# Two entries moved in a hand-written order: a scatter on GpSimd goes behind a weight split, a mask on VectorE goes behind a subtraction

## The chip, the core and the metric

One core of a Trainium2 chip runs the kernel. The metric is the device time of one execution in microseconds (us). The kernel before took 399.46 us (median of 3 runs, 399.36 to 399.62).

## The reference

Attention through a memory of 32 slots per head, and behind it a mixture of experts in which each row goes to one expert. All of it is float32; there are 8 batches of 8 heads, 576 rows, head size 64; the expert layer has width 512, 8 experts and 1024 hidden columns.

```python
a = exp(phi - max(phi, axis=rows)); a = a / (sum(a, axis=rows) + 1e-9)
k_m = einsum('bhsm,bhsd->bhmd', a, k); v_m = einsum('bhsm,bhsd->bhmd', a, v)
attn = softmax(q @ k_m^T / 8); x = (attn @ v_m) as 4608 rows of 512
logits = x @ w_gate; expert = argmax(logits); gate = softmax(logits)[expert]
out[row] = gate * (relu(x[row] @ w1[expert]) @ w2[expert])
```

## The kernel before

The 8 batches (0 to 7 in the code) go through the same stages and overlap: while TensorE is in the second expert layer of one batch, the other engines prepare the attention of the next. For each batch the kernel makes `phi`'s softmax and the memories `kvm` (line 308), turns the queries (`qT`, line 1029), makes the scores `sT` (line 451), their softmax and its transpose `eT` (lines 411 to 435), and from `eT` the gate's logits `lg` (line 494). A whole batch is then sent through one expert, the one that most of its rows choose, and its weights are loaded by a register's value. The rows that chose another expert, the strays, are written to lists in DRAM by indirect stores (one for each of the 5 row tiles of a batch, `send_stray`, line 610, GpSimd) and are done again at the end of the kernel.

The expert's matmuls run in pairs of a high and a low part. A second-layer tile of weights is loaded raw (`wraw`), ScalarE copies it to a rounded `whi`, and `wlo = wraw - whi` is the low part (`split`, lines 618 and 619; on GpSimd for most tiles, on VectorE for the rest). TensorE forms `whi*hh + wlo*hh + whi*hl` (line 768). In the first layer the weights are first multiplied with the value memory (`pu`, line 387, two PSUM buffers for each half of the hidden columns), ScalarE rounds each buffer to `uh` (line 391) and VectorE takes `ul = pu - uh` (line 394). PSUM has four buffers for such products, so a `pu` buffer can be written again only when its `uh` and its `ul` have been made.

What stands in which place is written by hand: `ORDER` is a list of step names, a batch digit and a step, and every engine issues its own instructions in the order in which the list makes them ("kept in order", at the end of the function). Nothing reorders them. The steps that matter here:

- `0Y0` to `0Y4`: the indirect stores of batch 0's strays, one row tile each, GpSimd.
- `1W3`: the split of the last second-layer tile of batch 1, `whi` on ScalarE and `wlo` on GpSimd.
- `20K3`, `21K3`: the softmax's subtraction of the row maximum for the two groups of heads of batch 2 (line 415); group 0's on GpSimd, group 1's on VectorE. `20L`, `21L` are the exponentials (line 418, ScalarE), `21M2` the scaling on GpSimd (line 432), `20M3`, `21M3` the transposes to `eT` (line 435, VectorE), `2R` the logits (line 494, TensorE).
- `1o03`: the second-layer product of row tile 0 with the weight tile of `1W3`.
- `3X2`: `stray_hot` of batch 3 (lines 565 and 567, VectorE): `hist` and the mask `soh`, which `3X5` on GpSimd reads (line 593).
- `3UH10`, `3UL10`, `3UH00`, `3UL00`: `uh` and `ul` of the first two `pu` buffers of batch 3, made by `3U0`; `3U1` makes the next two.

Of the kernel before, what the change touches and what calls it, by code (L numbers as in the profile page):

```python
# [31 lines left out]
0o41 0o22 0X2 0X5 10N 20C 2D 0o42 0o43 0y4 0z 1D2 1D1 3L1 1D3 3LQ 0o23 0y2 1U0 1UH00 1UH10 1UL10 1UL00 2E 1U1 1UH11  # L32
1UL11 1UH01 1UL01 1X5 1i00 1i01 1e01 1e00 0X6 0Y0 1i03 1e03 2FV 20F 21F 1i02 1e02 1i13 1e13 1i05 2G 2V 2G1 2V1 1W0
1i17 1e17 1W1 2J 20K1 21K 1e05 2V2 1i04 20K 1W2 00N 1i06 1e06 0Y3 1i16 1e16 1i07 1e07 21K1 20K2 21K2 1e04 21K3 20K3
0Y2 1W3 3L0 21L 21M 21M0 31A 20L 2V3 20M 20M0 20M1 20M2 21M1 1i11 1e11 20M3 31Q 1i12 1e12 21M2 21M3 21N 1o00 0align28
1o01 0align54 1o10 0align80 1o11 0align97 1o02 1o03 1o12 1o13 1y1 1i10 0CE1 1e10 2R 2R1 2R2 1i14 1e14 1i15 1o30 2R3 2X
2X3 2R4 2R6 2LW 1o31 1e15 2S1 1o32 1o33 2D1 1y3 2D3 1o20 1o21 1o22 1o40 1o41 30A 2T1 30A1 31A1 3A2 30B 2X4 30C 30Q 31B
0Y4 20N 1y0 2X2 2X1 31C 3D 1X6 2D0 2U0 2UH00 2UL00 2S0 2T0 2X5 2X6 2UH10 3E 1o42 1o23 2W3 30F 31F 2UL10 1o43 3FV 2i02
# [2 lines left out]
0align5 2o01 41A 2W2 0align31 2o02 0align57 2o03 31K1 2e12 31K2 31K3 30L 30M 2i16 2i15 2i10 0align108 2o10 30M0 2y0  # L41
30M1 31L 31M 31M0 30M2 30N 2e10 41A1 31M1 31M2 0Y1 31N 40A 30M3 2o11 2o12 31M3 3R 3R1 3R2 2i14 2o13 2e16 3R3 2o40 3X3
2y1 2o30 2o31 3R4 3R6 2e14 2e15 40A1 4A2 41B 2o20 2o21 2o32 2o33 2o22 3LW 3S0 3T0 3D0 3D1 40B 3X 2y3 3X4 3D3 5L0 3D2
40C 41C 4D 3X1 2Y2 3S1 3T1 41Q 40Q 2o41 2o42 2o43 2y4 2z 3U0 3UH10 3X2 0CZ 1Y3 3UL10 3UH00 3UL00 3W0 3X5 4E 41F 4FV
40F 3U1 3UH01 3UL01 3UH11 2o23 2y2 4G 4G1 4V 3i13 3UL11 3i15 3e15 3i02 3e13 3X6 3i03 4J 4V1 4V2 3e02 40K 40K1 40K2
3i01 40K3 3e03 4V3 3e01 41K 3i04 3i10 3e04 3W1 50A 41K1 3i06 3e06 3i05 3e05 3e10 3i00 3e00 41K2 3W2 2Y1 40L 40M 5LQ
50Q 3i11 3e11 3W3 40M0 40M1 3i16 3e16 3i07 3e07 41K3 41L 41M 3o00 0align0 3o01 0align26 3o02 3i14 3e14 0align65 3o10
# [1171 lines left out]
```

## Time and profile before

| | |
|---|---|
| median of 3 runs | 399.46 us (399.36 to 399.62) |
| the profiled execution | 399.74 us |
| span of that execution, first to last instruction | 398.1 us |
| mean granted TensorE clock | 0.998 of full speed |
| TensorE (PE) busy | 389.6 us, 98% of the span |
| VectorE (DVE) busy | 272.6 us, 68% |
| ScalarE (ACT) busy | 183.9 us, 46% |
| GpSimd (POOL) busy | 178.1 us, 45% |

The profile is one execution, taken by the hardware profiler. Its own time is 1.6 us longer than its span, and 0.28 us above the median of the runs. In a timeline each row has the start and the duration in us, the engine, the line, the operation, the tile written, the tiles read, and in brackets how long the engine had been idle before and what ended that. `PEld` is TensorE's weight load, which overlaps its matmuls. Matmuls are pipelined, so a matmul's duration is longer than the distance to the next one, and it is the distances between starts that tell whether TensorE lost time.

### The profile page before, as it was taken

The page shows a single profiled execution, that of the slowest core. Times are in us where ns is not written, and L with a number is a line of the kernel's source. Part 1 is how long each engine was busy: PE and PEld are TensorE (multiplying, and loading weights), DVE is VectorE, ACT ScalarE, POOL GpSimd, SP SyncE. Part 2 cuts the span into 40 slices and gives each one's busy share as a digit, 9 for nine tenths or more (in the row PEclk, how much of TensorE's full clock was granted, in tenths as well). Part 3 has the DMA queues.
Part 4 walks back from the last instruction along what each step waited for, and adds up shares of the span by engine and source line. Part 5 has one row for each costly group of instructions (what it writes and reads, how often), then busy time and mean ns, then how long its engine had stood idle before and what let it go on. Part 6 is the DMA issues. An engine that isn't in the chain of part 4 may idle for free.

```text
span 398.1 us, 11110 instructions
## 1 busy us (share of the span) xinstructions
PE 389.6 (98%) x4109; PEld 311.1 (78%) x4109; DVE 272.6 (68%) x719; ACT 183.9 (46%) x516; POOL 178.1 (45%) x268
## 2 busy tenths in 40 slices
PE   8889999999999999999999999999999999999995
PEld 4459777887877988798778887798788988698873
DVE  6899888578765866679646758668665876753313
ACT  3268433572357524664427534484337731371220
POOL 5358713367024530655312973364333747656010
PEclk9999999999999999999999999999999999999999
DMA  8998978991592947883487915787169114868313
GB/s 249 361 391 321 292 260 266 349 384 47 170 349 66 356 183 219 308 280 130 116 278 260 366 37 194 255 274 265 58 210 327 51 29 153 302 194 297 108 29 85
DMA packets 51032, 88.26 MB, mean 222 GB/s; under 512 B 7130, under 2 KB 15966, under 8 KB 50976
## 3 DMA queue, kind: packets, MB, share of 16 engines
q1 hardware_dynamic: 47552, 82.55, 61.2%
q0 software_dynamic: 2752, 4.75, 3.4%
q8 instruction: 35, 0.57, 0.6%
q10 hardware_dynamic: 672, 0.21, 0.2%
q14 instruction: 21, 0.17, 0.1%
HBM read 71.22 MB, written 16.48 MB: 220 GB/s over the span
## 4 chain that ended last, share of the span: by engine, by line
PE 75%; POOL 1%; DVE 0%; issue 0%
PE py L768 37%; PE ph L714 20%; PE py L667 6%; PE pu L387 3%; PE kvm L308 3%; PE sT L451 2%; PE lg L494 1%; POOL wlo L619 1%; PE py L653 1%; PE spy L938 0%; PE sph L918 0%; PE px L658 0%; PE sx L906 0%; POOL stray_list L610 0%; PE pk L346 0%; PE pg L367 0%
## 5 line engine op out<-in xcount | busy, mean ns | idle before, releaser
L768 PE MATMUL py<-whi,hh 128*128 128x512 f32 x256 | 101.3, 396 | 0.0
L768 PE MATMUL py<-wlo,hh 128*128 128x512 f32 x256 | 100.0, 391 | 0.2 <-POOL wlo L619 0.2
L768 PE MATMUL py<-whi,hl 128*128 128x512 f32 x256 | 99.8, 390 | 0.0
L648 DVE SCALAR_TENSOR_TENSOR hl<-ph,hh 128x224 fp32r<-128x224 f32 (+1 forms) x128 | 51.9, 416 | 42.4 <-ACT ht L645 25.7
L714 PE MATMUL ph<-eh,uh 128*128 128x288 f32 x252 | 77.2, 306 | 0.0
L714 PE MATMUL ph<-eh,ul 128*128 128x288 f32 x252 | 74.3, 295 | 0.0
L714 PE MATMUL ph<-el,uh 128*128 128x288 f32 x252 | 74.2, 295 | 0.0
L619 POOL TENSOR_TENSOR wlo<-wraw,whi 128x1024 fp32r<-128x1024 f32 x25 | 60.4, 2426 | 28.8 <-ACT whi L618 21.8
L645 ACT ACTIVATE hh<-ph 128x224 fp32r<-128x224 f32 (+1 forms) x128 | 47.7, 387 | 26.9 <-PE ph L714 26.4
L768 PEld LDWEIGHTS py<-whi,hh 128*128 128x128 f32 x256 | 48.0, 188 | 11.3 <-issue 2.0
L768 PEld LDWEIGHTS py<-whi,hl 128*128 128x128 f32 x256 | 48.0, 188 | 10.3
L768 PEld LDWEIGHTS py<-wlo,hh 128*128 128x128 f32 x256 | 48.1, 188 | 9.6 <-POOL wlo L619 0.6
L610 POOL DMA_INDIRECT stray_list<-pay,posi x40 | 42.1, 1053 | 23.5 <-issue 9.0
L714 PEld LDWEIGHTS ph<-eh,uh 128*128 128x128 f32 x252 | 47.3, 188 | 6.2 <-issue 1.2
L714 PEld LDWEIGHTS ph<-eh,ul 128*128 128x128 f32 x252 | 47.3, 188 | 0.3
L714 PEld LDWEIGHTS ph<-el,uh 128*128 128x128 f32 x252 | 47.3, 188 | 0.0
L783 ACT ACTIVATE y<-py,gw 128x512 f32<-128x512 f32 x31 | 21.2, 688 | 46.6 <-issue 27.4
L618 ACT CAST whi<-wraw 128x1024 fp32r<-128x1024 f32 x32 | 33.7, 1058 | 0.0
L553 POOL COPY gw<-gw 64x1 f32<-64x1 f32 x8 | 1.9, 236 | 68.6 <-DVE gw L547 68.6
L394 DVE TENSOR_TENSOR ul<-pu,uh 128x512 fp32r<-128x512 f32 x32 | 20.9, 682 | 16.3 <-ACT uh L391 16.2
L291 ACT ACTIVATE pT<-pT,nm 128x288 f32<-128x288 f32 x32 | 16.8, 528 | 11.8 <-DVE nm L286 11.8
L667 PE MATMUL py<-whi,ht 128*128 128x512 f32 x56 | 21.9, 391 | 0.0
(215 smaller groups left out, 586.9 us busy)
## 6 DMA issues: line engine op xcount, KB each, us to landing
wraw<-in_moe_w_dram SPq DMA_DIRECT2D x66, 512.0 KB, 5.9
kv<-in_v_dram SPq DMA_DIRECT2D x16, 576.0 KB, 7.6
out_dram<-y SPq DMA_DIRECT2D x141, 64.0 KB, 3.0
kv<-in_k_dram SPq DMA_DIRECT2D x14, 576.0 KB, 7.4
qt<-in_q_dram SPq DMA_DIRECT2D x10, 576.0 KB, 9.8
pt<-in_phi_dram SPq DMA_DIRECT2D x15, 288.0 KB, 6.4
ad<-s_t POOLq DMA_DIRECT2D x15, 288.0 KB, 3.5
sw<-in_moe_w_dram SPq DMA_DIRECT2D x6, 512.0 KB, 7.0
```

The costliest lines, as they stand in the source:

```text
L291: nc.scalar.activation(out=pT[:, j], in_=pT[:, j], func=AF.Exp, bias=nm[:, g, j:j + 1], scale=1.0, accum_out=zp[:, g, j:j + 1])
L308: nc.tensor.matmul(kvm[s][o0:o0 + 32, 0:2 * D], lhsT=as_[g][s0, j, c, :], rhs=kvs[g][s0, :, j, c, :], start=(c == 0), stop=(c == C - 1))
L394: nc.vector.tensor_tensor(out=ul[:, g, n0:n0 + DM], in0=pu[g, n0], in1=uh[:, g, n0:n0 + DM].bitcast(F32), op=ALU.subtract)
L610: nc.gpsimd.indirect_dma_start(out=ld_list[i][:, :], out_offset=bass.IndirectOffsetOnAxis(ap=posi[:, i:i + 1], axis=0), in_=pay[:, i, :], ...
L618: nc.scalar.copy(out=hi, in_=raw)
L619: eng.tensor_tensor(out=lo, in0=raw, in1=hi.bitcast(F32), op=ALU.subtract)
L645: nc.scalar.activation(out=hi, in_=ph, func=AF.Relu)
L648: nc.vector.scalar_tensor_tensor(out=lo, in0=ph, scalar=0.0, in1=hi.bitcast(F32), op0=ALU.max, op1=ALU.subtract)
L667: nc.tensor.matmul(o, lhsT=l, rhs=r, start=start, stop=stop)
L714: nc.tensor.matmul(ph, lhsT=lhs[:, g, fs], rhs=rhs[:, g, s0:s1], start=(n == 0), stop=(n == 5))
L768: nc.tensor.matmul(py, lhsT=lhs[:, f, i * P:i * P + P], rhs=rhs[:, f % 2, :], start=(f == 0 and n == 0), stop=(f == KF - 1 and n == 2))
L783: nc.scalar.activation(out=y, in_=v["py", i], func=AF.Copy, scale=gate)
```

## The change

Two entries of `ORDER` move. `0Y2` stood ahead of `1W3` and now stands behind it. `3X2` stood between `3UH10` and `3UL10` and now stands behind `3UL10`. Nothing else is changed.

```diff
-0Y2 1W3 3L0 21L 21M 21M0 31A 20L 2V3 ...
+1W3 0Y2 3L0 21L 21M 21M0 31A 20L 2V3 ...
...
-... 2z 3U0 3UH10 3X2 0CZ 1Y3 3UL10 3UH00 3UL00 3W0 3X5 4E 41F 4FV
+... 2z 3U0 3UH10 0CZ 1Y3 3UL10 3X2 3UH00 3UL00 3W0 3X5 4E 41F 4FV
```

On GpSimd, in batch 1's second layer (`stray_list` is the target of an indirect store, `s_t` the scores of batch 2):

```order
 L610 DMA stray_list_94<-pay,posi 21504x4
 L415 TENSOR_TENSOR s_t<-s_t,mm_1561 128x576
-L610 DMA stray_list_93<-pay,posi 21504x4
 L619 TENSOR_TENSOR wlo<-wraw_1237,whi 128x1024
+L610 DMA stray_list_93<-pay,posi 21504x4
 L432 TENSOR_TENSOR s_t<-s_t,ssum_1582 128x576
 L440 DMA ad<-s_t 128x576
```

The split now follows directly on the subtraction `20K3`, and the store stands between the split and `21M2`.

On VectorE, where the first layer of batch 3 begins (`y` is the end of batch 2's row tile 4, `hist` and `soh` are the step `3X2`):

```order
 L1029 STREAM_TRANSPOSE qT<-qt 128x1152 x2
 L683 SCALAR_TENSOR_TENSOR y<-py,gw,y 64x512
-L565 SCALAR_TENSOR_TENSOR hist<-em_117,es,hist 128x8
-L567 SCALAR_TENSOR_TENSOR soh<-em_117,es,ohr 128x40
-L394 TENSOR_TENSOR ul<-pu,uh 128x512 x4
+L394 TENSOR_TENSOR ul<-pu,uh 128x512
+L565 SCALAR_TENSOR_TENSOR hist<-em_117,es,hist 128x8
+L567 SCALAR_TENSOR_TENSOR soh<-em_117,es,ohr 128x40
+L394 TENSOR_TENSOR ul<-pu,uh 128x512 x3
 L648 SCALAR_TENSOR_TENSOR hl<-ph,hh 128x224
 L648 SCALAR_TENSOR_TENSOR ht<-ph,ht 128x64
```

Of the four `ul` the first now stands ahead of the two mask instructions, and the other three stay behind them. TensorE, ScalarE and SyncE have the same instructions in the same order as before.

## Rows read from the trace of the kernel before

**Rows 1.** The page: busy time by engine; the chain that ended last.

```profile
PE 389.6 (98%) x4109; PEld 311.1 (78%) x4109; DVE 272.6 (68%) x719; ACT 183.9 (46%) x516; POOL 178.1 (45%) x268
PE 75%; POOL 1%; DVE 0%; issue 0%
```

**Rows 2.** Timeline of all engines around 94 us: start us, us, engine, line, operation.

```profile
93.76 0.39 PE L768 MATMUL py<-whi,hh 128*128 128x512 f32 x1
...
94.44 0.39 PE L768 MATMUL py<-whi,hh 128*128 128x512 f32 x1
...
94.97 0.19 PEld L768 LDWEIGHTS py<-wlo,hh 128*128 128x128 f32 x1 [0.57 <-POOL wlo L619]
94.98 0.50 PE L768 MATMUL py<-wlo,hh 128*128 128x512 f32 x1 [0.15 <-POOL wlo L619]
...
95.54 0.40 PE L768 MATMUL py<-whi,hh 128*128 128x512 f32 x1
```

**Rows 3.** Timeline of POOL, 80 to 100 us.

```profile
88.74 1.04 POOL L610 DMA_INDIRECT stray_list<-pay,posi  x1 [0.30 <-issue]
89.78 1.20 POOL L415 TENSOR_TENSOR s_t<-s_t,mm 128x576 f32<-128x576 f32 x1
91.15 1.33 POOL L610 DMA_INDIRECT stray_list<-pay,posi  x1 [0.18 <-issue]
92.48 2.44 POOL L619 TENSOR_TENSOR wlo<-wraw,whi 128x1024 fp32r<-128x1024 f32 x1
96.42 1.16 POOL L432 TENSOR_TENSOR s_t<-s_t,ssum 128x576 f32<-128x576 f32 x1 [1.50 <-ACT ht L645]
```

**Rows 4.** Timeline of DVE, 86 to 99 us.

```profile
89.10 2.50 DVE L415 TENSOR_TENSOR s_t<-s_t,mm 128x576 f32<-128x576 f32 x1
...
98.94 0.76 DVE L435 STREAM_TRANSPOSE eT<-s_t 128x576 f32<-128x576 f32 x1
```

**Rows 5.** Lines 415 (DVE) and 619 (POOL) over the whole span: duration ns min/median/max.

```profile
L415 DVE TENSOR_TENSOR s_t<-s_t,mm x6: 744/758/2499, 89.1 to 321.3; 128x576 f32<-128x576 f32 x6
...
L619 POOL TENSOR_TENSOR wlo<-wraw,whi x25: 2379/2404/2929, 34.0 to 359.2; 128x1024 fp32r<-128x1024 f32 x25
```

**Rows 6.** Timelines of POOL and DVE in windows between 222 and 229 us.

```profile
222.58 2.40 POOL L619 TENSOR_TENSOR wlo<-wraw,whi 128x1024 fp32r<-128x1024 f32 x1
...
224.94 2.93 POOL L619 TENSOR_TENSOR wlo<-wraw,whi 128x1024 fp32r<-128x1024 f32 x1
...
224.65 0.95 DVE L415 TENSOR_TENSOR s_t<-s_t,mm 128x576 f32<-128x576 f32 x1
```

**Rows 7.** Timeline of PE, 98 to 104 us: the logits of batch 2.

```profile
99.84 0.74 PE L494 MATMUL lg<-eT,gm 128*32 128x160 f32 x16
```

**Rows 8.** Timeline of PE, 164.4 to 166 us: the second products of batch 3.

```profile
164.61 0.59 PE L387 MATMUL pu<-wraw,vT 64*32 64x512 f32 x1
164.62 0.27 PE L308 MATMUL kvm<-kv,pt 64*32 64x128 f32 x1
164.86 1.09 PE L387 MATMUL pu<-wraw,vT 64*32 64x512 f32 x15
165.88 0.50 PE L768 MATMUL py<-whi,hh 128*128 128x512 f32 x1
```

**Rows 9.** Timeline of DVE, 163 to 164.6 us.

```profile
163.20 0.70 DVE L683 SCALAR_TENSOR_TENSOR y<-py,gw,y 64x512 f32<-64x512 f32 x1
163.83 0.21 DVE L565 SCALAR_TENSOR_TENSOR hist<-em,es,hist 128x8 f32<-128x8 f32 x1
163.96 0.25 DVE L567 SCALAR_TENSOR_TENSOR soh<-em,es,ohr 128x40 f32<-128x40 f32 x1
164.13 0.67 DVE L394 TENSOR_TENSOR ul<-pu,uh 128x512 fp32r<-128x512 f32 x1
```

**Rows 10.** Timeline of PE, 211.75 to 213.1 us: the same place in batch 4.

```profile
211.88 0.27 PE L308 MATMUL kvm<-kv,pt 64*32 64x128 f32 x1
211.92 1.09 PE L387 MATMUL pu<-wraw,vT 64*32 64x512 f32 x12
212.94 0.40 PE L714 MATMUL ph<-eh,uh 128*128 128x288 f32 x1
```

**Rows 11.** Timeline of POOL at 169.4 us: the reader of the mask `soh`.

```profile
169.43 0.27 POOL L593 TENSOR_TENSOR pos<-pos,soh 128x40 f32<-128x40 f32 x1
```

More of the change, by code (lines that the diff above doesn't have):

```diff
@@ L34 @@
 1i17 1e17 1W1 2J 20K1 21K 1e05 2V2 1i04 20K 1W2 00N 1i06 1e06 0Y3 1i16 1e16 1i07 1e07 21K1 20K2 21K2 1e04 21K3 20K3
-0Y2 1W3 3L0 21L 21M 21M0 31A 20L 2V3 20M 20M0 20M1 20M2 21M1 1i11 1e11 20M3 31Q 1i12 1e12 21M2 21M3 21N 1o00 0align28
+1W3 0Y2 3L0 21L 21M 21M0 31A 20L 2V3 20M 20M0 20M1 20M2 21M1 1i11 1e11 20M3 31Q 1i12 1e12 21M2 21M3 21N 1o00 0align28
 1o01 0align54 1o10 0align80 1o11 0align97 1o02 1o03 1o12 1o13 1y1 1i10 0CE1 1e10 2R 2R1 2R2 1i14 1e14 1i15 1o30 2R3 2X
@@ L43 @@
 2y1 2o30 2o31 3R4 3R6 2e14 2e15 40A1 4A2 41B 2o20 2o21 2o32 2o33 2o22 3LW 3S0 3T0 3D0 3D1 40B 3X 2y3 3X4 3D3 5L0 3D2
-40C 41C 4D 3X1 2Y2 3S1 3T1 41Q 40Q 2o41 2o42 2o43 2y4 2z 3U0 3UH10 3X2 0CZ 1Y3 3UL10 3UH00 3UL00 3W0 3X5 4E 41F 4FV
+40C 41C 4D 3X1 2Y2 3S1 3T1 41Q 40Q 2o41 2o42 2o43 2y4 2z 3U0 3UH10 0CZ 1Y3 3UL10 3X2 3UH00 3UL00 3W0 3X5 4E 41F 4FV
 40F 3U1 3UH01 3UL01 3UH11 2o23 2y2 4G 4G1 4V 3i13 3UL11 3i15 3e15 3i02 3e13 3X6 3i03 4J 4V1 4V2 3e02 40K 40K1 40K2
```

## The prediction

> **What bounds the kernel now.** I read the page first. TensorE is busy for 98% of the span, and the chain of work that ended last, followed back from the end to 91 us, is TensorE's almost alone; one percent of the span in that chain is GpSimd's [rows 1]. So a change on GpSimd or VectorE pays only where TensorE stands still for it, and then at most what TensorE lost there. The second view is the timeline of TensorE. Behind 90 us I looked for places where two starts lie further apart than the same pair of instructions does elsewhere, and apart from patterns that come back in every batch there are two: one at 94.98 us, which the trace puts down to the split `wlo` on GpSimd [rows 2], and one at 164.86 us, inside the second products of batch 3 [rows 8]. The change touches exactly these two. The third view is the timeline of the engine that TensorE waits for at each, to see what stood ahead of the late instruction.
>
> **The first edit.** What TensorE loses: before the wait its starts lie (94.44 - 93.76) / 3 = 0.227 us apart. The three steps from 94.44 to 95.54 take 1.10 us where 3 x 0.227 = 0.68 would do, so 0.42 us are lost [rows 2]. That is more than the 0.15 us which the bracket gives as idle time, because matmuls overlap and the pipe has to fill again.
>
> Why `wlo` was late: GpSimd ends the subtraction `20K3` at 89.78 + 1.20 = 90.98, then spends 0.18 us on issue and 1.33 us on the store, and begins `wlo` only at 92.48, so that it ends at 94.92 [rows 3]. The weight load wanted it 0.57 us before 94.97, at 94.40 [rows 2]. With the store behind it, `wlo` can start at 90.98. Its inputs are old by then. Alone it takes 2.40 us [rows 5] and would end at 93.38. But it will not be alone: VectorE's subtraction `21K3` stands there from 89.10 to 91.60, 2.50 us for an instruction with a median of 0.76 [rows 4, 5]. It began in the shadow of GpSimd's subtraction and ended 0.62 us behind it, so I read it as waiting for GpSimd, and then running. The nearest rows for what comes next are those at 224 us: two splits stand back to back on GpSimd, VectorE's subtraction arrives 0.33 us before the first ends (222.58 + 2.40 = 224.98), it runs first and ends at 225.60, and the second split takes 2.93 instead of 2.40 us [rows 6]. Taking that value, `wlo` ends at 90.98 + 2.93 = 93.91, still 0.49 us before 94.40, and `21K3` ends at 91.60 as before. The stall goes: **-0.42 us**. Bounds: 0 if the time is lost again at the next thing that is late (below), and 0.42 at most, since TensorE cannot gain more here than it lost.
>
> What the store costs in its new place: with 0.18 us of issue and 1.04 to 1.33 us [rows 3] it runs from about 94.1 to at most 95.4. The next GpSimd instruction, the scaling `21M2`, had stood idle for 1.50 us and started at 96.42 because of something else [rows 3], so the store fits into that idle time: 0 us. If that cover were gone, it would be 1.3 us on the way to `eT`. Its list is read at the end of the kernel only. Nothing else is on that queue behind it except `21M2`.
>
> What is late next: the logits of batch 2. Their second half reads the last `eT` transpose, which ends at 98.94 + 0.76 = 99.70 [rows 4]. The 16 matmuls start over some 0.67 us from 99.84 on [rows 7], so the second half starts at about 100.17, and 0.42 us earlier it would be 99.75. That is only 0.05 us of slack, an estimate from these rows; the gain just fits.
>
> **The second edit.** Here the second buffer of `3U1` waits: the first matmul starts at 164.61, the next ones at 164.86, and the first subtraction `ul` ends at 164.13 + 0.67 = 164.80, 0.06 us earlier [rows 8, 9]. From the last `kvm` matmul to the next matmul that is not `pu` it takes 165.88 - 164.62 = 1.26 us; at the same place in batch 4, where nothing waits, 212.94 - 211.88 = 1.06 us [rows 8, 10]. So 0.20 us are lost. Without the two mask instructions ahead of it, `ul` starts where `hist` did, at 163.83 (0.30 us earlier), and ends at 164.50 [rows 9]. With the same 0.06 us that is 164.56, before TensorE asks at 164.61. The title of the change speaks of two subtractions, but the order shows the mask behind one; since the buffer waited for is that of the first, that is enough. **-0.20 us**; bounds 0 (another reader of the buffer holds it) and 0.25 (the whole distance from 164.61 to 164.86).
>
> The mask itself comes 0.6 us later; its reader on GpSimd starts at 169.43 [rows 11], five microseconds later: 0 us. The second `ul` keeps its place, since the sum of what stands ahead of it is the same.
>
> **The sum.** -0.42 - 0.20 = -0.62 us. The profiled execution would go from 399.74 to 399.12 us. It stands 0.28 us above the median of the runs, so I expect 399.46 - 0.62 = 398.84, say 398.85 us, 0.15% less. Changes within 0.2% (0.8 us) can hardly be told from none with a measurement of this kernel, so "the same" is the likeliest verdict although I expect a real gain.
>
> **The rivals.**
>
> GpSimd goes first, and it gets slower. When `20K3` ends at 90.98, either `21K3` or `wlo` goes on. In the kernel before, the issue gap of 0.18 us behind `20K3` let VectorE in; now a ready instruction of the same kind as `20K3` follows at once. Against VectorE speaks that `21K3` had waited since 89.10 and GpSimd's `20K3` still got in before it at 89.78 [rows 3, 4]; for VectorE speak the rows at 224 us, where the order of the same two kinds is exactly that of the changed kernel. If GpSimd wins, `21K3` ends at 93.38 + 0.62 = 94.00, 2.40 us later. The chain behind it (exponential, sum, scaling, transpose) has no idle time of that size, so `eT` ends at 102.10 and the logits' second half waits from 99.75 until then, 1.93 us behind the 100.17 of before. With the -0.20 of the second edit that is +1.7 us, 401.2 us. It decides from a delay of 0.05 + 0.62 = 0.67 us of `21K3` on: below that there is still a gain. Chance 0.12.
> The Trainium skill ("SBUF — State Buffer", section on the two separate sides of SBUF) has a rule on this: VectorE operations with two SBUF inputs and GpSimd operations share a pair of ports, whichever starts first holds it for its whole instruction, and the other blocks fully. The trace agrees that one blocks (2.50 against 0.76 us), but the rule does not say which of two waiting ones starts first, and so leaves this rival open.
>
> Only a part arrives. The slack of 0.05 us at the logits is less than nothing if the transposes move by a little, and what TensorE wins at 94 us is then given back at 100 us: 399.46 - 0.20 = 399.25 us. Or the buffer of the second products is held by something else, and only the first edit pays: 399.05 us. For it speaks that TensorE runs at 98% and any small wait shows; against it, that most of what it waits for later is released by its own earlier work and moves along. Chance 0.23 together.
>
> More than the sum. The raw tile is freed a microsecond earlier (93.91 against 94.92), so the loads that follow start earlier, and TensorE may find one of its smaller waits gone too. No row shows a wait of that size for such a load behind 90 us, so I give it 0.08; it would be some 398.4 us.
>
> **How the numbers follow.** Both edits pay: 0.57, from 398.55 to 399.05 us with the spread of the runs (0.13 us either way). Faster by over 0.2% means below 398.66: all of the last rival and about a fifth of the forecast's own spread, with something for what I did not see, 0.22. Slower by over 0.2%, above 400.26: GpSimd first, 0.12. The rest, 0.66, is the same. The range goes from 398.35 (more than the sum) to 399.75 (nothing gained, plus the spread of the runs) and leaves out that rival and little else.
>
> **What would show it.** In the profile of the changed kernel GpSimd goes from `s_t` (line 415) to `wlo` (line 619) with no store between, `wlo` takes about 2.9 us and ends near 93.9, and VectorE's subtraction still ends near 91.6. TensorE's starts around 94.7 lie 0.23 us apart with no bracket of `wlo`. The logits start near 99.4. At 164 us `ul` precedes `hist`, and from the last `kvm` to the next product it takes about 1.06 us. I am wrong if VectorE's line 415 ends near 94 and the logits wait for `eT`; if the wait of TensorE moves to another place and the span shrinks by less than 0.3 us; or if the second products still show a step of 0.25 us.

## The result: 2 us slower, by the rival and not by the forecast

The changed kernel took 401.51 us (median of 6 runs, 401.22 to 402.6), the kernel before 399.54 us beside it (6 runs, 399.36 to 399.77): a ratio of 1.0053, with a 95% interval from 1.004 to 1.0066. The forecast was 398.85 us. The rival in which GpSimd goes first, priced at 401.2 us, is what happened. The profiled execution shown here took 402.6 us, with a span of 400.8 us. (One experiment below, the one with no issue ahead, was profiled in an execution 5 us longer at a granted clock of 0.981; its rows are read for order and durations only.)

On the page, TensorE's busy time and the chain that ended last, which answer to [rows 1], hardly tell the two kernels apart. The chain has 2% less of TensorE, and 1% each of VectorE and issue. What stands out is VectorE's busy time, 2.5 us more than before; one subtraction that waits, shown below, makes 2.35 us of it, since its wait counts as busy:

```profile
PE 390.1 (97%) x4109; PEld 310.8 (78%) x4109; DVE 275.1 (69%) x719; ACT 183.6 (46%) x516; POOL 178.0 (44%) x268
...
PE 73%; DVE 1%; issue 1%; POOL 1%; ACT 0%
```

The timeline of TensorE (start us, us, engine, line, operation, and in brackets the idle time before it and what ended it) shows what went and what came:

```profile
94.68 0.39 PE L768 MATMUL py<-whi,hh 128*128 128x512 f32 x1
94.91 0.39 PE L768 MATMUL py<-wlo,hh 128*128 128x512 f32 x1
...
98.53 0.39 PE L768 MATMUL py<-whi,hl 128*128 128x512 f32 x1
99.38 0.37 PE L714 MATMUL ph<-eh,uh 128*128 128x288 f32 x1 [0.46 <-DVE ht L648]
...
100.34 0.47 PE L494 MATMUL lg<-eT,gm 128*32 128x160 f32 x8
102.32 0.47 PE L494 MATMUL lg<-eT,gm 128*32 128x160 f32 x8 [1.52 <-DVE eT L435]
```

The stall that the first edit was aimed at is gone: the product with `wlo` starts 0.23 us behind its neighbour, without a bracket, where [rows 2] had one. But two waits are new. TensorE stands idle for 0.46 us because a first-layer buffer comes free too late, and the logits, one run of 16 in [rows 7], fall into two halves with 1.98 us between their starts.

GpSimd's and VectorE's timelines, which answer to [rows 3, 4], say why:

```profile
88.98 1.02 POOL L610 DMA_INDIRECT stray_list<-pay,posi  x1 [0.30 <-DMA kv<-in_k_dram]
90.03 1.17 POOL L415 TENSOR_TENSOR s_t<-s_t,mm 128x576 f32<-128x576 f32 x1
91.15 2.41 POOL L619 TENSOR_TENSOR wlo<-wraw,whi 128x1024 fp32r<-128x1024 f32 x1
93.73 1.33 POOL L610 DMA_INDIRECT stray_list<-pay,posi  x1 [0.18 <-issue]
...
89.33 4.85 DVE L415 TENSOR_TENSOR s_t<-s_t,mm 128x576 f32<-128x576 f32 x1
...
101.51 0.76 DVE L435 STREAM_TRANSPOSE eT<-s_t 128x576 f32<-128x576 f32 x1
```

VectorE's subtraction `21K3` now takes 4.85 us and ends at 94.18. That is 0.62 us behind the end of `wlo` (91.15 + 2.41 = 93.56), as it ended 0.62 us behind the end of `20K3` before. VectorE stood by for two GpSimd instructions instead of one, and got in where GpSimd made its next pause, 0.18 us ahead of the store. In the kernel before that pause stood directly behind `20K3`, because the store did. By moving the store, the change moved the one opening that VectorE had.

ScalarE's timeline shows how a late subtraction becomes two waits:

```profile
94.26 0.69 ACT L418 ACTIVATE s_t<-s_t 128x576 f32<-128x576 f32 x1 [6.15 <-POOL wlo L619]
...
97.50 0.34 ACT L645 ACTIVATE hh<-ph 128x224 fp32r<-128x224 f32 x1
```

It stands idle for 6.15 us before the exponential of what VectorE subtracted. (The bracket names `wlo`, the last thing to end by the profile; the exponential reads `21K3`'s result.) Behind it on ScalarE's queue stand the copies of the first-layer products, and only when VectorE has used them is the buffer free that TensorE wants at 99 us. The exponential, sum, scaling and transpose follow with nothing to give, and `eT` ends at 102.27.

At the second place, VectorE and then TensorE, which answer to [rows 8, 9]:

```profile
166.32 0.69 DVE L394 TENSOR_TENSOR ul<-pu,uh 128x512 fp32r<-128x512 f32 x1 [0.20 <-ACT uh L391]
166.93 0.21 DVE L565 SCALAR_TENSOR_TENSOR hist<-em,es,hist 128x8 f32<-128x8 f32 x1
...
167.34 0.27 PE L308 MATMUL kvm<-kv,pt 64*32 64x128 f32 x1
167.34 1.13 PE L387 MATMUL pu<-wraw,vT 64*32 64x512 f32 x12
168.40 0.50 PE L768 MATMUL py<-whi,hh 128*128 128x512 f32 x1
```

`ul` precedes `hist`, and from the last `kvm` to the next product it takes 168.40 - 167.34 = 1.06 us, as the prediction wanted. But 1.7 us earlier TensorE's weight loads show a pause that the trace of before does not have:

```profile
165.64 1.71 PEld L308 LDWEIGHTS kvm<-kv,pt 64*32 64x32 f32 x117 [0.38 <-issue]
```

The balance against before goes by starts of TensorE's matmuls, since the idle time in a bracket is less than what is lost. For the buffer's wait it needs one more row of the kernel before, the last product ahead of the logits:

```profile
98.74 0.39 PE L768 MATMUL py<-whi,hl 128*128 128x512 f32 x1
```

Up to the logits it is -0.42 (the stall), +0.71 (the buffer: from the last product to the logits 100.34 - 98.53 = 1.81 us, before 99.84 - 98.74 = 1.10) and +1.71 (the logits: 1.98 us between the halves, where 0.74 - 0.47 = 0.27 is the cost of eight more matmuls), together +2.00 us. The medians differ by 401.51 - 399.54 = 1.97 us.

The two profiled executions differ by more, 400.8 - 398.1 = 2.7 us in their spans. The other 0.7 us lie elsewhere: 0.24 us in the first 21 us, ahead of both places; 0.31 us from the logits to the end of the second place, where the pause costs more than the second edit's 0.20 us gives; and 0.20 us near 336 us, where two weight loads wait 0.27 and 0.24 us for `hh` and `hl` as they don't in the trace of before. What of these the executions without a profile have is not shown.

### The profile page after: what moved, and what is told of

Same layout as the page of the kernel before. It is cut to its first block, busy times and chain, and to the rows that moved or that the text cites. A ratio compares the mean times of both kernels' runs of the same rounds, so it can differ in the third digit from the quotient of the medians.

```text
span 400.8 us, 11110 instructions
## 1 busy us (share of the span) xinstructions
PE 390.1 (97%) x4109; PEld 310.8 (78%) x4109; DVE 275.1 (69%) x719; ACT 183.6 (46%) x516; POOL 178.0 (44%) x268
## 4 chain that ended last, share of the span: by engine, by line
PE 73%; DVE 1%; issue 1%; POOL 1%; ACT 0%
PE py L768 36%; PE ph L714 20%; PE py L667 6%; PE pu L387 3%; PE kvm L308 3%; PE sT L451 2%; PE lg L494 1%; POOL wlo L619 1%; PE py L653 1%; PE spy L938 0%; PE sph L918 0%; PE px L658 0%; DVE ssum L422 0%; PE sx L906 0%; DVE eT L435 0%
## 5 line engine op out<-in xcount | busy, mean ns | idle before, releaser
L391 ACT CAST uh<-pu 128x512 fp32r<-128x512 f32 x32 | 17.2, 590 | 10.5 <-PE pu L387 10.4
```

What stands on the lines that cost most here:

```text
L391: nc.scalar.copy(out=uh[:, g, n0:n0 + DM], in_=pu[g, n0])
```

## The experiments

Each is compared with runs of the kernel before on the same chip. The ratios and their 95% intervals are those on record; they are not the quotients of the two medians beside them, and can differ from these by some 0.1%. Two questions: which edit costs the time, and what decides whether VectorE or GpSimd goes first.

**One edit at a time.** First the store alone:

```diff
-... 21K3 20K3 0Y2 1W3 3L0 ...
+... 21K3 20K3 1W3 0Y2 3L0 ...
```

> The first edit alone (the store 0Y2 behind the split 1W3; the mask 3X2 stays where it was before). Theory 'GpSimd runs on': all of the loss comes from this edit, VectorE's subtraction of line 415 near 89 us takes about 4.9 us, the logits of batch 2 wait about 1.8 us for eT, and the time is 2.0 to 2.4 us above the kernel before (0.5 to 0.6%). Rival 'other cause': if the time lies within 0.3 us of the kernel before, the loss needs the second edit or comes from something outside of both places.

Measured: 402.0 us against 399.95, ratio 1.0048 (1.0029 to 1.0066). VectorE's subtraction took 4.82 us and the second half of the logits again waited 1.52 us for `eT`. Then the mask alone:

```diff
-... 3UH10 3X2 0CZ 1Y3 3UL10 3UH00 ...
+... 3UH10 0CZ 1Y3 3UL10 3X2 3UH00 ...
```

> The second edit alone (the mask 3X2 behind 3UL10; the store stays where it was before). Theory: VectorE's ul of batch 3 starts 0.3 us earlier, the step of 0.25 us inside the second products goes, and the time falls by 0.2 us (0.05%), which can hardly be told from none. From the last kvm to the first product that is not pu it takes 1.06 us where it was 1.26. Rival 'another reader holds the buffer': the 1.26 us stay. A loss of over 0.5 us would speak for the second edit as a cause of the slower time.

Measured: 399.77 against 399.95 us, ratio 0.9999 (0.9984 to 1.0014); VectorE's subtraction took 2.50 us as before. So the first edit makes the whole loss, and the second makes nothing that these runs can tell from zero.

**More stores behind the split.** If VectorE is kept out because a store stands ahead, taking away the store ahead (`0Y3`) should let it in:

```diff
-... 1i06 1e06 0Y3 1i16 ... 20K3 1W3 0Y2 3L0 ...
+... 1i06 1e06 1i16 ... 20K3 1W3 0Y2 0Y3 3L0 ...
```

> The changed kernel, with the store 0Y3 moved too: it stood ahead of GpSimd's subtraction 20K3 and now stands behind the split and 0Y2, so that 20K3 and the split 1W3 run back to back with no store ahead of them. VectorE's subtraction 21K3 then arrives in the middle of 20K3, as at 224 us in the kernel before. Theory A 'it is the store ahead of the run that lets GpSimd keep VectorE out': VectorE gets in behind 20K3, its subtraction takes 1.0 to 1.3 us, the split about 2.9 us, both stalls are gone and the time is 0.6 us below the kernel before (0.15%). Theory B 'GpSimd runs on through any row of instructions that are ready': VectorE waits until the split ends near 92.3 us, its subtraction takes about 3.6 us, the logits wait about 0.6 us and the time is 0.4 to 1.0 us above the kernel before.

Measured: 400.4 us, ratio 1.0013 (0.9999 to 1.0028). VectorE was still kept out until `wlo` had ended, at 88.97 + 2.40 = 91.37, plus 0.62:

```profile
87.20 0.62 POOL L440 DMA_DIRECT2D ad<-s  x1
87.85 1.17 POOL L415 TENSOR_TENSOR s_t<-s_t,mm 128x576 f32<-128x576 f32 x1
88.97 2.40 POOL L619 TENSOR_TENSOR wlo<-wraw,whi 128x1024 fp32r<-128x1024 f32 x1
...
88.47 3.52 DVE L415 TENSOR_TENSOR s_t<-s_t,mm 128x576 f32<-128x576 f32 x1
```

So it is not the indirect store as such. What I saw in these rows only later is that now another DMA issue, the plain store of `ad` (step `00N`), stood directly ahead of the run.

**One store between.** The opening put back, with the other store in it:

```diff
-... 1i06 1e06 0Y3 1i16 ... 20K3 1W3 0Y2 3L0 ...
+... 1i06 1e06 1i16 ... 20K3 0Y3 1W3 0Y2 3L0 ...
```

> The changed kernel, with the store 0Y3 moved from ahead of 20K3 to between 20K3 and the split 1W3; 0Y2 stays behind the split. There is again a gap of issue behind 20K3, as in the kernel before, but the split comes one store earlier than there. Both theories A and B: VectorE gets in at that gap, its subtraction takes 1.0 to 1.5 us, the split ends near 93.8 us, 0.6 us before it is wanted, both stalls are gone and the time is 0.6 us below the kernel before (0.15%). If VectorE's subtraction still takes over 3 us, a gap of issue is not what lets it in.

Measured: 399.46 against 399.95 us, ratio 0.9975 (0.9948 to 1.0001).

```profile
87.95 1.17 POOL L415 TENSOR_TENSOR s_t<-s_t,mm 128x576 f32<-128x576 f32 x1
89.30 1.37 POOL L610 DMA_INDIRECT stray_list<-pay,posi  x1 [0.17 <-DMA kv<-in_k_dram]
90.68 2.42 POOL L619 TENSOR_TENSOR wlo<-wraw,whi 128x1024 fp32r<-128x1024 f32 x1
...
88.60 1.15 DVE L415 TENSOR_TENSOR s_t<-s_t,mm 128x576 f32<-128x576 f32 x1
...
98.92 0.74 PE L494 MATMUL lg<-eT,gm 128*32 128x160 f32 x16
```

VectorE gets in at the pause of 0.17 us ahead of the store and ends at 89.75, again 0.62 to 0.63 us behind GpSimd's subtraction; the logits are one run again. `wlo` is early as well, since one store fewer stands ahead of the whole group: this order has the gain without the loss. It was run twice more, first beside a second copy of the kernel before:

> The kernel before, unchanged, with a profile of its own beside those of the variants. The profiles of the changed kernel and of four variants all show a step of 0.4 us inside the kvm matmuls of batch 3 that the first profile of the kernel before does not have. If the step belongs to the execution and not to the edits, it is here too, and the variants are to be compared with this profile. Time: the same as before within 0.2%. VectorE's subtraction near 89 us takes 2.5 us again.

> The version with one store between 20K3 and the split, again, for a tighter interval. Both theories: 0.6 to 1.0 us below the kernel before (0.15 to 0.25%); the logits of batch 2 wait for nothing.

Measured: the copy 399.41 against 399.46 us (0.9999, 0.9974 to 1.0024), the version 398.64 (0.9981, 0.9955 to 1.0008).

> The version with one store between GpSimd's subtraction and the split, once more. By the sum of its parts: VectorE's subtraction of batch 2 takes 1.15 us, no wait in the logits, 0.5 to 0.8 us below before (0.998 to 0.9988). Rival, that the earlier runs were scatter: within 0.2 us of before.

Measured: 399.39 against 399.91 us (0.9994, 0.998 to 1.0009). Its median is lower in all three, by 0.49, 0.82 and 0.52 us, and no interval stands clear of 1. It beats the changed kernel plainly, the kernel before only probably.

**The two instructions by themselves.** A small kernel leaves out the reference's work and stores zeros: GpSimd does a subtraction and two splits back to back, while VectorE's subtraction comes up.

```python
nc.gpsimd.tensor_tensor(out=w, in0=dl, in1=ma.broadcast_to([P, 18, M]), op=ALU.subtract)
for j in range(2):
    nc.gpsimd.tensor_tensor(out=lo, in0=raw, in1=hi.bitcast(F32), op=ALU.subtract)
nc.vector.tensor_tensor(out=s_b, in0=s_b, in1=mb.broadcast_to([P, 18, M]), op=ALU.subtract)
```

> The reference's work is left out; zeros are stored. Twelve cases, one after the other: GpSimd runs a two-input subtraction (short: 576 columns, about 1.2 us; long: 1024 columns, about 2.4 us) and behind it two splits of 1024 columns. VectorE's two-input subtraction of 576 columns (0.76 us alone) arrives while the first one runs. In the cases 'early' the splits have been ready long before; in 'mid' the first split becomes ready, by a copy on ScalarE, only while the first subtraction runs. Theory B1 'GpSimd runs on through what was already waiting in its queue when the present instruction began, and lets VectorE in where the next became ready only later' (it fits 94 us, and 224 us where the split's input was made 0.8 us into the split before): early: VectorE takes 4 to 7 us, until both splits are done, however late it arrives; mid: VectorE gets in behind the first subtraction and takes 0.9 to 2.5 us. Rival B2 'the length or the time of arrival decides' (at 224 us the running instruction was a long one and VectorE came 0.3 us before its end): short: VectorE is kept out, early or mid; long with a late arrival: VectorE gets in, early or mid.

Measured: in all 12 cases VectorE got in behind the instruction that ran when it came, in 1.12 to 2.16 us. Both theories fell, and what was left was a difference between this kernel and the real one: here no DMA issue stood ahead of GpSimd's run. At 224 us of the kernel before, where VectorE got in too [rows 6], none stands directly ahead either. Three experiments put this to the test, each in its own way. The small kernel, with a GpSimd DMA issue ahead:

```diff
+nc.gpsimd.dma_start(out=g, in_=z.rearrange("p t m -> p (t m)"))
 nc.gpsimd.tensor_tensor(out=w, in0=dl, in1=ma.broadcast_to([P, 18, M]), op=ALU.subtract)
```

> The reference's work is left out; the output is zeros. Eleven cases in turn: GpSimd does a short subtraction of two inputs (576 columns) and two splits of two inputs (1024 columns) back to back, and VectorE's subtraction of two inputs comes up while the first of them runs. Ahead of GpSimd's run stands nothing (2 cases), an issue of a plain DMA (4), an issue of an indirect DMA (4), or an issue of a DMA with an idle gap behind it (1). If it is a GpSimd DMA issue directly ahead that keeps VectorE out: with none or a gap VectorE's subtraction takes 1.1 to 2.2 us and the next split 2.8 to 2.9; behind an issue VectorE's ends only with GpSimd's second split, 4 to 7 us, and both splits take 2.3 to 2.4. Rival, that it is not the DMA: all eleven take 1.1 to 2.2 us.

Two cases in the timelines of GpSimd (L83 is the issue, L86 the subtraction, L89 the splits) and of VectorE (L93), with nothing ahead and with an indirect issue:

```profile
6.26 1.16 POOL L86 TENSOR_TENSOR w<-dl,ma 128x576 f32<-128x576 f32 x1 [5.29 <-DVE ma L77]
7.37 5.15 POOL L89 TENSOR_TENSOR lo<-raw,hi 128x1024 fp32r<-128x1024 f32 x2
...
60.21 0.99 POOL L83 DMA_INDIRECT g<-z,idx  x1 [2.96 <-DVE z L72]
61.22 1.18 POOL L86 TENSOR_TENSOR w<-dl,ma 128x576 f32<-128x576 f32 x1
62.34 4.64 POOL L89 TENSOR_TENSOR lo<-raw,hi 128x1024 fp32r<-128x1024 f32 x2
...
6.60 1.43 DVE L93 TENSOR_TENSOR s_b<-s_b,mb 128x576 f32<-128x576 f32 x1
...
61.24 6.37 DVE L93 TENSOR_TENSOR s_b<-s_b,mb 128x576 f32<-128x576 f32 x1
```

With nothing ahead VectorE took 1.43 and 1.42 us. Behind an issue, plain or indirect, it took 5.95 to 6.92 us and ended about 0.62 us behind the second split. Two of the eleven cases test nothing: VectorE took 0.74 us in each, because it came before the reduction behind `ma` had ended, which GpSimd's subtraction waits for. To come ahead of that subtraction is not enough by itself:

```profile
50.46 1.02 POOL L83 DMA_INDIRECT g<-z,idx  x1 [1.68 <-DVE z L72]
...
50.96 6.92 DVE L93 TENSOR_TENSOR s_b<-s_b,mb 128x576 f32<-128x576 f32 x1
```

Here `ma` was done, and VectorE came while GpSimd was still at the issue, 0.54 us ahead of the start of GpSimd's subtraction (51.50); it was kept out all the same. The case meant to have an idle gap had none (0.02 us between issue and subtraction) and took 6.25 us like the others. I had said 4 to 7 us for these.

In the real kernel, no DMA issue ahead: both `0Y3` and `00N` moved behind the split, everything else as in the changed kernel.

```diff
-... 1W2 00N 1i06 1e06 0Y3 1i16 ... 20K3 1W3 0Y2 3L0 ...
+... 1W2 1i06 1e06 1i16 ... 20K3 1W3 0Y2 0Y3 00N 3L0 ...
```

> Change, with batch 0's third store and the plain store of its scores' copy (the line of ad) also moved behind the split, so that GpSimd issues no DMA shortly ahead of its subtraction and the split. If a DMA issue directly ahead keeps VectorE out: VectorE's subtraction of batch 2 takes about 1.0 us, the split about 2.9 instead of 2.4, the second half of the logits does not wait, and the time is 0.3 to 0.7 us below before (ratio 0.998 to 0.999). Rival, that any run of ready instructions in this place keeps VectorE out: its subtraction takes 3.5 us or more, as with three behind, and the time is 0.3 to 1.0 us above before (1.001 to 1.0025).

Measured: 399.43 against 399.92 us, ratio 0.999 (0.9969 to 1.001).

```profile
93.11 1.16 POOL L415 TENSOR_TENSOR s_t<-s_t,mm 128x576 f32<-128x576 f32 x1 [0.34 <-DVE mm L411]
94.23 2.93 POOL L619 TENSOR_TENSOR wlo<-wraw,whi 128x1024 fp32r<-128x1024 f32 x1
...
93.97 0.92 DVE L415 TENSOR_TENSOR s_t<-s_t,mm 128x576 f32<-128x576 f32 x1
```

These are the numbers that the prediction had taken from 224 us: VectorE in 0.92 us, the split in 2.93. The order of the two instructions is the changed kernel's; what stands ahead differs. (GpSimd was idle for 0.34 us ahead of its subtraction: a run with no issue directly ahead begins behind idle time, here as in the small kernel, so the two are one condition in these runs.) And the reverse, in the kernel before: a store put ahead of two of the three splits at 224 us.

```diff
-4e12 51K1 4W1 4W0 5V2 ... 1Y0 3Y3 4Y3 ...
+4e12 51K1 4W1 3Y3 4W0 5V2 ... 1Y0 4Y3 ...
```

> Before, with one store of batch 3 moved from behind GpSimd's three splits of 220 to 228 us to between the first and the second of them. If a DMA issue ahead keeps VectorE out of what follows: VectorE's subtraction there (0.95 us in before, in between the second and third split) ends only with the third split, about 3.5 to 4.5 us, and the third split takes 2.4 instead of 2.9; batch 5's softmax is late by about 2.5 to 3 us and the time is 1 to 2.5 us above before (1.0025 to 1.006). Rival: VectorE still gets in behind the split that runs when it comes (0.9 to 2.5 us), and the time is within 0.5 us of before.

Measured: 402.56 against 399.92 us, ratio 1.0075 (1.0053 to 1.0096), 2.64 us where I had put 1 to 2.5. GpSimd, VectorE, TensorE:

```profile
222.35 1.07 POOL L610 DMA_INDIRECT stray_list<-pay,posi  x1 [0.16 <-issue]
223.43 4.74 POOL L619 TENSOR_TENSOR wlo<-wraw,whi 128x1024 fp32r<-128x1024 f32 x2
...
224.22 4.59 DVE L415 TENSOR_TENSOR s_t<-s_t,mm 128x576 f32<-128x576 f32 x1
...
231.41 0.50 PE L768 MATMUL py<-whi,hh 128*128 128x512 f32 x1 [1.37 <-DVE hl L648]
```

The subtraction that took 0.95 us in [rows 6] takes 4.59, and TensorE waits 1.37 us for `hl`, which stands behind it on VectorE's queue. The last small kernel asks what ends the effect:

```diff
 nc.gpsimd.dma_start(out=g, in_=z.rearrange("p t m -> p (t m)"))
+nc.gpsimd.memset(y, 0.0)
 nc.gpsimd.tensor_tensor(out=w, in0=dl, in1=ma.broadcast_to([P, 18, M]), op=ALU.subtract)
```

> The reference's work is left out; the output is zeros. Twelve cases as before, a plain GpSimd DMA issue ahead of a short subtraction and two splits (four, in two or three cases), with VectorE's subtraction of two inputs coming up during the first of them; between the issue and the run stands an idle gap of some 0.2 to 1.5 us (1, 2, 3 or 8 short VectorE reductions that GpSimd's subtraction waits behind), a GpSimd memset, or a GpSimd copy of one input. If what an issue leaves behind ends with GpSimd's first idle gap: VectorE gets in at 1.1 to 2.2 us behind an idle gap, and is kept out (4 us or more) behind the memset and the copy; with four splits behind an issue it is kept out until the fourth ends, 9 to 11 us. Rival, that it is a matter of time since the issue: the longer gap, the memset and the copy let it in, and of four splits behind an issue it waits for the first two or three only (under 8 us).

Three of its twelve cases (L76 the plain issue, L84 the memset, L89 the subtraction, L92 the splits; VectorE L96): the shortest idle gap, a memset between, and four splits directly behind an issue.

```profile
23.69 0.56 POOL L76 DMA_DIRECT2D g<-z  x1 [2.99 <-DVE z L72]
24.33 1.15 POOL L89 TENSOR_TENSOR w<-dl,ma 128x576 f32<-128x576 f32 x1
...
52.41 0.36 POOL L84 MEMSET y<- 128x288 f32 x1
52.71 1.17 POOL L89 TENSOR_TENSOR w<-dl,ma 128x576 f32<-128x576 f32 x1
...
84.88 1.17 POOL L89 TENSOR_TENSOR w<-dl,ma 128x576 f32<-128x576 f32 x1
85.99 9.22 POOL L92 TENSOR_TENSOR lo<-raw,hi 128x1024 fp32r<-128x1024 f32 x4
...
24.68 1.42 DVE L96 TENSOR_TENSOR s_b<-s_b,mb 128x576 f32<-128x576 f32 x1
...
52.60 6.49 DVE L96 TENSOR_TENSOR s_b<-s_b,mb 128x576 f32<-128x576 f32 x1
...
84.78 11.05 DVE L96 TENSOR_TENSOR s_b<-s_b,mb 128x576 f32<-128x576 f32 x1
```

An idle gap of GpSimd ends it, down to the shortest that was tried: 24.33 - 24.25 = 0.08 us, and VectorE takes 1.42 us, as with nothing ahead; so do the longer gaps. A memset between (6.49 and 6.23 us) or a copy (6.03 us) does not end it. Nor does time: behind an issue VectorE stood by for 11.05 us, until the fourth split was done. All of it is as the first theory said (11.05 us where I had put 9 to 11); the rival, that it is a matter of time since the issue, falls.

## Why the prediction was wrong

**The step that failed** is the one on who goes next at 90.98 us: "the nearest rows for what comes next are those at 224 us". They were nearest in the two instructions and not in what stood ahead of them. At 224 us no DMA issue stood directly ahead of GpSimd's run; at 89.78 the subtraction stood directly behind a store, its start at the store's end [rows 3]. The runs show that this decides: without an issue ahead the changed order gives 0.92 us for VectorE, with one 4.85; and a store put at 224 us turns 0.95 into 4.59. The prediction also misread a row there: `21K3` did not begin "in the shadow of GpSimd's subtraction" but at 89.10, 0.68 us ahead of it, while GpSimd was at the store; so it had lost to an instruction that began later. The right rows stood in the prediction, in the rival: `21K3` had come at 89.10, ahead of `20K3`, and had not been let in, and "the issue gap of 0.18 us" had let it in later. I weighed that against the rows at 224 us and gave it 0.12. As the bounds of that step I took 0 and -0.42, so the unknown order had no end on the side of a loss, though the working of the rival had the price of one.

**The rival's price held.** It gave an end of `21K3` 2.40 us later; 4.85 - 2.50 = 2.35 came. It put the second half of the logits 1.93 us later than before; by the balance it was -0.42 + 0.71 + 1.71 = 2.00. The wait at the buffer I had not seen, because I followed the softmax's chain and not ScalarE's queue behind the exponential. It added nothing of its own: the second half starts 0.05 us behind the end of `eT` (102.32 against 102.27), and VectorE's timeline shows no idle time from 97.63 us up to that transpose, so without the wait at the buffer the one at the logits would have been longer. The rival gave 401.2 us, and 401.51 came.

**The stall behind `wlo`** went as predicted (-0.42), and `wlo` took 2.41 us and not 2.93, since nobody came between. **The late store** cost nothing: the scaling on GpSimd was idle for 3.94 us ahead of its start at 99.00 and still had time. **The slack of 0.05 us** at the logits was not put to the test, by the change or by an experiment: the version with one store between kept the logits in one run with `wlo` early, but there VectorE's subtraction took 1.15 us where it had taken 2.50, so `eT` came earlier too.

**The second edit** did what was said in the order, and `pu`'s step of 0.20 us is not there. Whether it pays is another matter. The pause of 0.35 to 0.38 us in the weight loads of `kvm` stands in the profile of the change and in that of most experiments, among them two that change something else and leave this place as it was (the store alone, and the store at 224 us). Where it stands, `ul` is ready in time even in the old order, and the step is gone without the edit. The profiles of the kernel before and of its copy have the step and no pause; one of the new version has neither, and there TensorE gained 0.2 us more over the copy at this place. So the -0.20 holds in some executions and is zero in others, and 0.9999 (0.9984 to 1.0014) agrees with anything between. What makes the pause is open.

## What to carry to other kernels

When two engines share a resource, look not only at the pair that collides, but at what stands ahead of it on the engine that holds: an issue gap that looks like waste (0.18 us ahead of a store) can be the only opening the other engine gets. Before you close up a run of GpSimd instructions behind a DMA that GpSimd issued, ask which VectorE instruction with two SBUF inputs comes up during it; in these runs it waited for the whole run. Take a row as the price of an unseen order only if its neighbours ahead match too, and let an order that you don't know reach to both sides of the range.

## What the runs showed of the hardware

GpSimd instructions that follow a DMA issue of GpSimd without an idle gap, up to five in a row here, kept VectorE's subtraction of two SBUF inputs out for their whole length (11.05 us for one that takes 0.74 to 0.76 us alone). The first idle gap, 0.08 us in the small kernel and 0.17 to 0.18 us ahead of a store in the real one, let it in, and it ended 0.62 us later; gaps of 0.02 to 0.03 us did not. Without a DMA issue ahead it got in behind the GpSimd instruction that ran when it came, and the next split took 2.85 to 2.93 us instead of 2.33 to 2.44. A plain and an indirect issue acted alike; a GpSimd memset or copy in between did not end it.

The issue alone does not keep VectorE out. In the kernel before, a VectorE subtraction of two SBUF inputs (line 1088) runs in 0.72 us beside an issue that GpSimd follows with an idle gap:

```profile
325.46 1.01 POOL L610 DMA_INDIRECT stray_list<-pay,posi  x1 [0.16 <-issue]
...
326.04 0.72 DVE L1088 TENSOR_TENSOR el<-eT,eh 128x576 fp32r<-128x576 f32 x1
```

The Trainium skill ("SBUF — State Buffer", section "SBUF: two separate sides") says that of a VectorE operation with two SBUF inputs and a GpSimd operation that reads SBUF, whichever starts first gets the shared pair of ports for its whole instruction. With nothing ahead on GpSimd the runs agree. Behind a DMA issue they do not: VectorE lost though its row starts 0.68 us ahead of GpSimd's subtraction (89.10 and 89.78 in the kernel before), and it was kept out not for an instruction but for a whole run (9.22 us of splits and the 1.17 us ahead of them); the measurement decides.

The Trainium skill ("Perfetto Trace Analysis", section "DMA Instruction — SWDGE (GPSIMD)") says that two of GpSimd's processors take the place of the hardware that otherwise makes up a DMA. If the others went on to the next instruction meanwhile, that instruction would have the ports before the issue's row ends, and the instructions behind would overlap without a break until an idle gap brings the processors together. That would fit the rows, but no run here looks inside GpSimd, and it stays a guess.
